# A spectral block with a gated MLP: an addition moved behind its copy, the weights' sums moved ahead of a multiplication, the banks read at the head of a step, and one transform stage a step later

## The chip, the cores and the metric

The kernel runs on one core of one Trainium2 chip. The metric is the device time of one execution in microseconds (us). Before the change it is 1405.28 us, the median of 3 runs (1405.17 to 1407.20).

## The reference

```python
xn = _layernorm(x, axis=-1)
return x + _A_ref(xn, A_w_r, A_w_i) + _B_ref(xn, B_w_gate, B_w_up, B_w_down)

# _A_ref: a global filter in the frequency domain
X = rfft2(x) * (w_r + 1j * w_i);  y = irfft2(X, s=(S, D))
# _B_ref: a gated MLP
h = sigmoid(x @ w_gate) * (x @ w_up);  return h @ w_down
```

x has S = 2048 rows and D = 576 columns, the MLP is F = 4608 wide, and all of it is in fp32. The kernel splits every fp32 operand of a multiplication into a high and a low part (in the type fp32r) for TensorE, and adds three partial products.

## The kernel before

The program has two large parts. The first computes h = sigmoid(xn Wg) * (xn Wu); the second computes h Wd and, beside it, the whole spectral branch.

**The units.** Both products with xn use Strassen's scheme with seven products in place of eight. A unit (f, p) handles one block of 128 columns of Wg and of Wu and one of the two halves p of the rows; f runs over 36 blocks. `unit` (line 388) is written in the order in which the engines get their work. A product (`prod`, line 355) is seven matmuls of 128x512. TensorE (PE) runs P5 into the bank pE, P6 into pB, P2 into pA, P7 into pB, P1 of the next unit into its own pA (`ahead`, line 384), P4 into pB and P3 into pE, which has two banks. ScalarE (ACT) reads between the products: the copy pB <- pA (line 396), the copy h[:,0] (line 400), the gate's sigmoid g[:,0] (line 403), the copy h[:,1] (line 406) and the second sigmoid (line 413). VectorE (DVE) adds pE to h[:,1] (line 410), later pE to h[:,0] (line 416), and multiplies h by g (line 417). P3 accumulates into the bank pE that the addition of line 410 reads, so P3 waits for that addition.

Seven times in a unit, between these steps, `beside` is called. It gives one step each to three generators of side work: `make_w`, which splits the next block's weights (ScalarE's copies on line 213, the low parts on lines 217 and 219) and forms the sums that Strassen's scheme needs (lines 229, 231, 232); `early`, for the last unit only, which fetches and splits the first operands of the second part; and the sides, which are `export` (line 420) and `make_t` (line 447). `export` forms the sums of h in place (lines 434 to 443) and stores them to a buffer in DRAM; `make_t` does the same for w_down (low parts on line 462). A unit with p = 0 uses weights that were split during the units before; in a unit with p = 1 the next block's weights are still being split. An instruction that waits holds back all that stands behind it on its engine.

**The product stage.** The second part is a list of 252 steps (line 1214 on): 7 products j, 2 halves p, and 18 blocks k of the sum. A step has twelve matmuls of 128x288 into the four banks m0 to m3 (`down`, line 1197). Ahead of them stand, in this order, a fetch of the operand of ten steps later, its split into a high part on ScalarE (`cut_hi`, line 795, four steps ahead of use) and a low part on DVE (`cut_lo`, line 799, three steps ahead), and `emptied`, which reads the banks of a finished product (`evac`, lines 1141 and 1145). When k comes to its end, the next product wants the same four banks.

**The spectral branch** runs beside these steps, as generators that get one step each in `aside`, behind the matmuls. `phase1b` (line 917) handles one block of 128 rows: it normalizes (xb, line 285), transposes on PE (pf, lines 940 and 941), copies out (fh, fl), multiplies (pd, line 962), copies out on ScalarE in four parts (ah) and subtracts on DVE (al), multiplies again (pa, line 975), copies out (x1, ScalarE) and stores x1 to DRAM. Sixteen blocks begin at the steps 2 + int(3.7 i), so three or four steps apart, and up to five are under way at a time. pf, pd and pa share two pairs of PSUM banks (tag pp); ah, al and x1 have one buffer each. The later phases use the same pairs.

From the third unit on the order on PE, DVE and ScalarE is the order of the program text; only the first two units are ordered by the framework. Line numbers below are those of the kernel before where nothing else is said.

Of the kernel before, what the change touches and what calls it, by code (L numbers as in the profile page):

```python
# [9 lines left out]
F32 = mybir.dt.float32  # L10
F32R = mybir.dt.float32r
I32 = mybir.dt.int32
AF = mybir.ActivationFunctionType
OP = mybir.AluOpType
PSUM = bass.MemoryType.PSUM

P = 128
# [107 lines left out]
def spectral_glu_kernel(ctx: ExitStack, tc: tile.TileContext, x, w_r, w_i, w_gate, w_up, w_down, out):  # L125
# [59 lines left out]
    def get_x(p, k):  # L185
        return X[p, HOME.get(k, k)]
# [20 lines left out]
    def weight(f, k):  # L207
        i, n = WPLACE[k]
        return WS[f, i][:, n]
# [142 lines left out]
    STEPS = ((0, 0), (3, 0), (0, 3), (1, 1), (4, 1), (1, 4), (2, 2))  # L352
    H = {}

    def prod(b, w, xx, start, stop, skip=False):
        for j, (sx, sw) in enumerate(STEPS):
            nc.tensor.matmul(b, w[:, sw, :], xx[:, sx, :], start=start and j == 0, stop=stop and j == len(STEPS) - 1,  # L357
                             skip_group_check=skip)

# [16 lines left out]

    B = {}

    def made(u, b, k, start, stop=True):
        f, p = u  # L380
        ka, kb = FACTORS[k]
        prod(B[u, b], weight(f, kb), get_x(p, ka), start, stop, not start)

    def ahead(u):
        B[u, "A"] = bank("bA", f"pA{u[0]}_{u[1]}", 2)
# [2 lines left out]
    def unit(u, beside, after):  # L388

        f, p = u  # L390
        h = new_h(f, p)
        g = run.tile([P, 2, CW], F32, tag="g", name=f"g{f}_{p}")
        B[u, "B"] = bank("bB", f"pB{f}_{p}")
        B[u, "E"] = bank("bE", f"pE{f}_{p}", 2)
        bA, bB, bE = (B[u, k] for k in "ABE")
        nc.scalar.activation(bB, bA, AF.Copy)
        made(u, "E", "P5", True)
        beside()
        made(u, "B", "P6", False)
        nc.scalar.activation(h[:, 0], bB, AF.Copy)  # L400
        beside()
        made(u, "A", "P2", False)
        nc.scalar.activation(g[:, 0], bA, AF.Sigmoid)
        beside()
        made(u, "B", "P7", False)
        nc.scalar.activation(h[:, 1], bB, AF.Copy)  # L406
        beside()
        if after:
            ahead(after)
        nc.vector.tensor_tensor(h[:, 1], h[:, 1], bE, op=OP.add)  # L410
        beside()
        made(u, "B", "P4", False)
        nc.scalar.activation(g[:, 1], bB, AF.Sigmoid)  # L413
        beside()
        made(u, "E", "P3", False)
        nc.vector.tensor_tensor(h[:, 0], h[:, 0], bE, op=OP.add)  # L416
        nc.vector.tensor_tensor(h, h, g, op=OP.mult)  # L417
        beside()

    def export(k, p):  # L420

        a, b = H[2 * k, p], H[2 * k + 1, p]
        A11, A21, A12, A22 = a[:, 0], a[:, 1], b[:, 0], b[:, 1]

        def put(what, src):
            nc.sync.dma_start(ssp[ORDER.index(what)][p][k], src)

        put("P1", A11)
        put("P2", A12)
        put("P4", A22)  # L430
        s = run.tile([P, 2, CW], F32, tag="s", name=f"s{k}_{p}")
        S1, S2 = (s[:, i] for i in range(2))
        yield
        nc.vector.tensor_tensor(S1, A21, A22, op=OP.add)
        put("P5", S1)
        yield
        nc.vector.tensor_tensor(S2, S1, A11, op=OP.subtract)
        put("P6", S2)
        yield
        nc.vector.tensor_tensor(A21, A11, A21, op=OP.subtract)  # L440
        put("P7", A21)
        yield
        nc.vector.tensor_tensor(A12, A12, S2, op=OP.subtract)
        put("P3", A12)
        yield

    def make_t(k):
# [353 lines left out]
    def early():  # L801
        for n in range(20):
            if n < 2:
                for i in range(3):
                    fetch(3 * n + i)
            else:
                fetch_t(0, n - 2)
            if 12 <= n <= 12 + CA:
                cut_hi(n - 12)
            if 13 <= n < 13 + CA:  # L810
                cut_lo(n - 13)
            yield
        for n in range(FS, FA):
            fetch(n)
# [5 lines left out]
    for i, u in enumerate(UNITS):  # L820
# [29 lines left out]

        unit(u, beside, after)
        if f % 2 == 1:
            sides.append(export(f // 2, p))
        if u == (3, 0):
            load_raw(4)
            load_raw(5)
# [60 lines left out]
    def phase1b(t):  # L917
# [50 lines left out]
        yield  # L968
        for o, sl, src in quarters:
            lo(al[o, sl, :], src, ah[o, sl, :])  # L970
        yield
        pa = pair(f"pa{t}")
        for sl in range(2):
# [232 lines left out]

    done, out_of = [], []

    def emptied():
        out_of[:] = [g for g in out_of if next(g, out_of) is not out_of]  # L1210
        out_of.extend(g for g in done if next(g, done) is not done)
        done.clear()

    for n, (j, p, k) in enumerate(seq):
        fetch(n + FA)
        for load in loads.pop(n, []):
            load()
        if n:
            cut_hi(n + CA)
            cut_lo(n + CA - 1)  # L1220
        emptied()
        if k in (0, NPR - 2):
            for m in range(2):
                down(n, m)
                down(n + 1, m)
        elif k in (1, NPR - 1):
            for m in range(2, TPC):
                down(n - 1, m)
                down(n, m)
        else:  # L1230
            for m in range(TPC):
                down(n, m)
        active.extend(b() for b in begin.pop(n, []))
        aside()
    while active or done or out_of:
        emptied()
        aside()
    assert not begin and not loads, (begin, loads)
    written.close()
# [22 lines left out]
```

## Time and profile before

| what | us |
|---|---|
| median of 3 runs | 1405.28 (1405.17 to 1407.20) |
| the profiled execution: its own time | 1405.81 |
| the profiled execution: span of the profile | 1403.9 |
| PE busy (share of the span) | 1379.7 (98%) |
| DVE busy | 967.0 (69%) |
| ScalarE (ACT) busy | 714.8 (51%) |

The span runs from the first to the last instruction that the profiler recorded; the execution's own time is 1.9 us longer. All traced times are places or durations in this one execution. A row of instructions gives the place where it starts, how long it takes, the engine, the line, the operation, the tiles that are written and read, the shape, and a count where several alike stand behind one another; in brackets stands the idle time of the engine just ahead of it and what ended it. A row of the waits gives the total, the number of waits and the longest. A row of windows gives the stretch, its length, the busy time of PE, PEld (the weight load), DVE, ScalarE, GpSimd and SyncE with the instructions in brackets, the granted clock of PE, the busy share of the transfer engines and GB/s.

### The profile page before, as it was taken

The numbers are of one execution on the slowest core, as the hardware profiler recorded it, in microseconds if no ns is written. First come the engines' busy times: TensorE is split into PE (matmuls) and PEld (weight loads), VectorE is DVE, ScalarE is ACT, GpSimd is POOL, SyncE is SP. The second block draws the span as 40 slices with busy tenths as digits, with TensorE's granted clock in tenths as the row PEclk, the third lists the DMA queues.
The fourth block names the chain that finished last, engine by engine and source line by source line (L and its number), as shares of the span: only waits on it lengthen the run. The fifth ranks groups of instructions, "written<-read, shape, count | busy, mean of one in ns | idle before, by whom it ended". The sixth has DMA issues, their size and how long they took to land.

```text
span 1403.9 us, 22607 instructions
## 1 busy us (share of the span) xinstructions
PE 1379.7 (98%) x7827; PEld 1220.9 (87%) x7827; DVE 967.0 (69%) x1807; ACT 714.8 (51%) x1469; POOL 12.7 (1%) x29
## 2 busy tenths in 40 slices
PE   9999999999999999999999999999999999999999
PEld 7778888788887888888788878999999999999998
DVE  8795677666866677666867665666757777756664
ACT  5564444444444444444444433655657767745553
POOL 2000000000000000000000000000000000000000
PEclk9999999999999999999999999999999999999999
DMA  7022565456554565545564439996899999988751
GB/s 242 23 99 92 181 215 206 159 172 211 188 206 147 188 206 206 178 168 204 187 208 157 169 143 335 329 331 216 257 293 276 308 282 306 306 284 278 246 189 62
DMA packets 221538, 296.77 MB, mean 211 GB/s; under 512 B 18544, under 2 KB 124400, under 8 KB 221168
## 3 DMA queue, kind: packets, MB, share of 16 engines
q1 hardware_dynamic: 221280, 295.26, 63.5%
q8 instruction: 62, 1.02, 0.3%
q14 instruction: 52, 0.43, 0.1%
q10 hardware_dynamic: 144, 0.07, 0.0%
HBM read 177.82 MB, written 117.44 MB: 210 GB/s over the span
## 4 chain that ended last, share of the span: by engine, by line
PE 86%; DVE 9%; issue 2%; DMA 2%; ACT 2%; DVEq 0%; ACTq 0%; SPq 0%
PE m L1203 26%; PE pB L357 21%; PE pE L357 15%; PE pA L357 14%; PE pd L962 2%; PE pe L1091 2%; PE py L1054 1%; PE pa L975 1%; PE pb L1006 1%; PE pc L1028 1%; DMA acc<-in_A_x 1%; DVE xs L323 1%; DVE raw L229 1%; DVE w L217 1%; PE pz L1069 0%
## 5 line engine op out<-in xcount | busy, mean ns | idle before, releaser
L1203 PE MATMUL m<-tt,sp 128*128 128x288 f32 x3024 | 415.9, 294 | 4.5 <-DVE u L1141 2.8
L1203 PEld LDWEIGHTS m<-tt,sp 128*128 128x128 f32 x3024 | 403.2, 188 | 5.8 <-DVE u L1141 3.5
L799 DVE TENSOR_TENSOR sp<-sf,sp 128x512 fp32r<-128x512 f32 x252 | 169.2, 688 | 24.4 <-ACT sp L795 22.1
L795 ACT ACTIVATE sp<-sf 128x512 fp32r<-128x512 f32 x252 | 155.2, 629 | 48.9 <-PE m L1203 25.7
L213 ACT ACTIVATE w<-raw 128x384 fp32r<-128x384 f32 x238 | 113.2, 515 | 99.8 <-DVE raw L229 98.8
L357 PE MATMUL pA<-X1A,w 128*128 128x512 f32 x518 | 129.2, 389 | 0.0
L357 PE MATMUL pE<-X1S,w 128*128 128x512 f32 x490 | 123.4, 392 | 4.2 <-DVE h L410 4.1
L416 DVE TENSOR_TENSOR h<-h,pE 128x512 f32<-128x512 f32 x68 | 46.8, 688 | 108.9 <-PE pE L357 108.8
L357 PE MATMUL pE<-X0S,w 128*128 128x512 f32 x483 | 121.1, 390 | 0.1
L357 PE MATMUL pB<-X1S,w 128*128 128x512 f32 x476 | 120.7, 393 | 0.1
L357 PE MATMUL pA<-X0A,w 128*128 128x512 f32 x483 | 120.8, 389 | 0.0
L357 PE MATMUL pB<-X0S,w 128*128 128x512 f32 x476 | 119.2, 390 | 1.0 <-ACT h L400 1.0
L357 PEld LDWEIGHTS pA<-X1A,w 128*128 128x128 f32 x518 | 97.2, 188 | 20.1
L357 PEld LDWEIGHTS pE<-X1S,w 128*128 128x128 f32 x490 | 91.1, 188 | 26.7 <-DVE h L410 8.0
L357 PEld LDWEIGHTS pB<-X1S,w 128*128 128x128 f32 x476 | 88.1, 188 | 23.3 <-ACT h L400 4.5
L357 PEld LDWEIGHTS pE<-X0S,w 128*128 128x128 f32 x483 | 90.4, 188 | 19.6 <-DVE w L217 0.5
L357 PEld LDWEIGHTS pA<-X0A,w 128*128 128x128 f32 x483 | 90.6, 188 | 18.9
L413 ACT ACTIVATE g<-pB 128x512 f32<-128x512 f32 x68 | 40.7, 598 | 130.0 <-PE pB L357 130.0
L357 PEld LDWEIGHTS pB<-X0S,w 128*128 128x128 f32 x476 | 89.2, 188 | 19.9 <-ACT h L400 1.4
L400 ACT ACTIVATE h<-pB 128x512 f32<-128x512 f32 x68 | 40.1, 589 | 120.9 <-PE pB L357 116.2
L410 DVE TENSOR_TENSOR h<-h,pE 128x512 f32<-128x512 f32 x68 | 46.6, 685 | 74.5 <-ACT h L406 74.5
L417 DVE TENSOR_TENSOR h<-h,g 128x1024 f32<-128x1024 f32 x68 | 83.3, 1225 | 7.4 <-DVE h L416 0.5
(206 smaller groups left out, 1907.3 us busy)
## 6 DMA issues: line engine op xcount, KB each, us to landing
sf<-ss SPq DMA_DIRECT2D x252, 256.0 KB
ss<-h SPq DMA_DIRECT2D x180, 256.0 KB
ts<-tP SPq DMA_DIRECT2D x126, 288.0 KB
tt<-ts SPq DMA_DIRECT2D x126, 288.0 KB
ss<-s SPq DMA_DIRECT2D x72, 256.0 KB
wd<-in_B_w_down SPq DMA_DIRECT2D x36, 288.0 KB
raw<-in_B_w_gate SPq DMA_DIRECT2D x72, 128.0 KB
raw<-in_B_w_up SPq DMA_DIRECT2D x72, 128.0 KB
```

Of the source, the lines that this page charges most:

```text
L213: nc.scalar.activation(o[:, i, :3, :], src[:, i], AF.Copy)
L357: nc.tensor.matmul(b, w[:, sw, :], xx[:, sx, :], start=start and j == 0, stop=stop and j == len(STEPS) - 1, skip_group_check=skip)
L400: nc.scalar.activation(h[:, 0], bB, AF.Copy)
L410: nc.vector.tensor_tensor(h[:, 1], h[:, 1], bE, op=OP.add)
L413: nc.scalar.activation(g[:, 1], bB, AF.Sigmoid)
L416: nc.vector.tensor_tensor(h[:, 0], h[:, 0], bE, op=OP.add)
L417: nc.vector.tensor_tensor(h, h, g, op=OP.mult)
L795: nc.scalar.activation(s[:, 0], SF[n], AF.Copy)
L799: nc.vector.tensor_tensor(SP_[n][:, 1], SF[n], f32(SP_[n][:, 0]), op=OP.subtract)
L962: nc.tensor.matmul(pd[:, e, :NQ], l, r, start=n == 0, stop=n == len(steps) - 1)
L1091: nc.tensor.matmul(pe[:, e, :NQ], l, r, start=n == 0, stop=n == len(steps) - 1)
L1203: nc.tensor.matmul(o, s[:, a, m * P:(m + 1) * P], t[:, b, :], start=k == 0 and i == 0, stop=k == NPR - 1 and i == 2)
```

## The change

In `unit` the addition to h[:,1] moves from behind P1 of the next unit to directly behind ScalarE's copy h[:,1], ahead of that place's `beside`. The seventh `beside` moves from behind the addition to h[:,0] and the multiplication to ahead of both, directly behind P3. In the last unit, which has no next one, P2 is split: four matmuls stand in its place, and the other three and the sigmoid g[:,0] stand behind P7, where other units have the next P1.

`export` of the last unit writes P3's operand into a tile of its own in place of h's buffer, and `early` splits one more low part. In the product stage the first step of a bank's reading (`read_out`) stands ahead of the step's `cut_hi` and `cut_lo`; the steps of readings that were begun earlier stay behind them. `phase1b` has one more step between al and pa. The line numbers of the changed kernel are up to 9 higher.

```diff
@@ -352,8 +352,9 @@
     STEPS = ((0, 0), (3, 0), (0, 3), (1, 1), (4, 1), (1, 4), (2, 2))
     H = {}
 
-    def prod(b, w, xx, start, stop, skip=False):
-        for j, (sx, sw) in enumerate(STEPS):
+    def prod(b, w, xx, start, stop, skip=False, which=range(len(STEPS))):
+        for j in which:
+            sx, sw = STEPS[j]
             nc.tensor.matmul(b, w[:, sw, :], xx[:, sx, :], start=start and j == 0, stop=stop and j == len(STEPS) - 1,
                              skip_group_check=skip)
 
@@ -376,10 +377,10 @@
 
     B = {}
 
-    def made(u, b, k, start, stop=True):
+    def made(u, b, k, start, stop=True, which=range(len(STEPS))):
         f, p = u
         ka, kb = FACTORS[k]
-        prod(B[u, b], weight(f, kb), get_x(p, ka), start, stop, not start)
+        prod(B[u, b], weight(f, kb), get_x(p, ka), start, stop, not start, which)
 
     def ahead(u):
         B[u, "A"] = bank("bA", f"pA{u[0]}_{u[1]}", 2)
@@ -399,25 +400,31 @@
         made(u, "B", "P6", False)
         nc.scalar.activation(h[:, 0], bB, AF.Copy)
         beside()
-        made(u, "A", "P2", False)
-        nc.scalar.activation(g[:, 0], bA, AF.Sigmoid)
+        if after:
+            made(u, "A", "P2", False)
+            nc.scalar.activation(g[:, 0], bA, AF.Sigmoid)
+        else:
+            made(u, "A", "P2", False, which=range(4))
         beside()
         made(u, "B", "P7", False)
         nc.scalar.activation(h[:, 1], bB, AF.Copy)
+        nc.vector.tensor_tensor(h[:, 1], h[:, 1], bE, op=OP.add)
         beside()
         if after:
             ahead(after)
-        nc.vector.tensor_tensor(h[:, 1], h[:, 1], bE, op=OP.add)
+        else:
+            made(u, "A", "P2", False, which=range(4, len(STEPS)))
+            nc.scalar.activation(g[:, 0], bA, AF.Sigmoid)
         beside()
         made(u, "B", "P4", False)
         nc.scalar.activation(g[:, 1], bB, AF.Sigmoid)
         beside()
         made(u, "E", "P3", False)
+        beside()
         nc.vector.tensor_tensor(h[:, 0], h[:, 0], bE, op=OP.add)
         nc.vector.tensor_tensor(h, h, g, op=OP.mult)
-        beside()
-
-    def export(k, p):
+
+    def export(k, p, apart=False):
 
         a, b = H[2 * k, p], H[2 * k + 1, p]
         A11, A21, A12, A22 = a[:, 0], a[:, 1], b[:, 0], b[:, 1]
@@ -440,8 +447,9 @@
         nc.vector.tensor_tensor(A21, A11, A21, op=OP.subtract)
         put("P7", A21)
         yield
-        nc.vector.tensor_tensor(A12, A12, S2, op=OP.subtract)
-        put("P3", A12)
+        o = run.tile([P, 2, CW], F32, tag="g", name=f"o{k}_{p}")[:, 0] if apart else A12
+        nc.vector.tensor_tensor(o, A12, S2, op=OP.subtract)
+        put("P3", o)
         yield
 
     def make_t(k):
@@ -807,7 +815,7 @@
                 fetch_t(0, n - 2)
             if 12 <= n <= 12 + CA:
                 cut_hi(n - 12)
-            if 13 <= n < 13 + CA:
+            if 13 <= n <= 13 + CA:
                 cut_lo(n - 13)
             yield
         for n in range(FS, FA):
@@ -850,7 +858,7 @@
 
         unit(u, beside, after)
         if f % 2 == 1:
-            sides.append(export(f // 2, p))
+            sides.append(export(f // 2, p, not after))
         if u == (3, 0):
             load_raw(4)
             load_raw(5)
@@ -968,6 +976,7 @@
         yield
         for o, sl, src in quarters:
             lo(al[o, sl, :], src, ah[o, sl, :])
+        yield
         yield
         pa = pair(f"pa{t}")
         for sl in range(2):
@@ -1206,19 +1215,24 @@
 
     done, out_of = [], []
 
-    def emptied():
-        out_of[:] = [g for g in out_of if next(g, out_of) is not out_of]
-        out_of.extend(g for g in done if next(g, done) is not done)
+    def read_out():
+        fresh = [g for g in done if next(g, done) is not done]
         done.clear()
+        return fresh
+
+    def emptied(fresh):
+        out_of[:] = [g for g in out_of if next(g, out_of) is not out_of] + fresh
 
     for n, (j, p, k) in enumerate(seq):
         fetch(n + FA)
         for load in loads.pop(n, []):
             load()
+        fresh = read_out()
         if n:
             cut_hi(n + CA)
+        if n > 1:
             cut_lo(n + CA - 1)
-        emptied()
+        emptied(fresh)
         if k in (0, NPR - 2):
             for m in range(2):
                 down(n, m)
@@ -1233,7 +1247,7 @@
         active.extend(b() for b in begin.pop(n, []))
         aside()
     while active or done or out_of:
-        emptied()
+        emptied(read_out())
         aside()
     assert not begin and not loads, (begin, loads)
     written.close()
```

What DVE has behind a unit with p = 0 and in the unit with p = 1 that follows it: h_0_2010 is the first unit's h, raw are the weights of the next block, and the sums of lines 229, 231 and 232 are those for which ScalarE's copies wait. Before:

```order
L217 TENSOR_TENSOR w_6_2042<-raw_1915,w_6_2042 128x3x256
L219 TENSOR_TENSOR w_6_2042<-raw_1915,w_6_2042 32x3x128
L416 TENSOR_TENSOR h_0_2010<-h_0_2010,pE_0_2013 128x512
L417 TENSOR_TENSOR h_0_2010<-h_0_2010,g_0_2011 128x1024
L229 TENSOR_TENSOR raw_1915<-raw_1915 128x2x384
L231 TENSOR_TENSOR raw_1915<-raw_1915 128x384
L232 TENSOR_TENSOR raw_1915<-raw_1915 128x384
L462 TENSOR_TENSOR tP_2113<-wd_2044,tP_2113 128x288
```

and now:

```order
L217 TENSOR_TENSOR w_6_2042<-raw_1915,w_6_2042 128x3x256
L219 TENSOR_TENSOR w_6_2042<-raw_1915,w_6_2042 32x3x128
L229 TENSOR_TENSOR raw_1915<-raw_1915 128x2x384
L424 TENSOR_TENSOR h_0_2010<-h_0_2010,pE_0_2013 128x512
L425 TENSOR_TENSOR h_0_2010<-h_0_2010,g_0_2011 128x1024
L231 TENSOR_TENSOR raw_1915<-raw_1915 128x384
L232 TENSOR_TENSOR raw_1915<-raw_1915 128x384
L470 TENSOR_TENSOR tP_2113<-wd_2044,tP_2113 128x288
```

The first sum of the weights has moved ahead of the addition to h[:,0] (line 416, now 424) and of the multiplication (417, now 425). Further on in the same unit with p = 1, whose h is h_1_2096, the rows up to its addition to h[:,0]; w_6 is a low part of the weights, s_0 and h_0 belong to an export, tP to `make_t`. Before:

```order
L437 TENSOR_TENSOR s_0_2118<-s_0_2118,h_0_1822 128x512
L217 TENSOR_TENSOR w_6_2127<-raw_1915,w_6_2127 128x2x256
L219 TENSOR_TENSOR w_6_2127<-raw_1915,w_6_2127 32x2x128
L462 TENSOR_TENSOR tP_2144<-wd_2046,tP_2144 128x288
L440 TENSOR_TENSOR h_0_1822<-h_0_1822 128x512
L410 TENSOR_TENSOR h_1_2096<-h_1_2096,pE_1_2099 128x512
L443 TENSOR_TENSOR h_0_2010<-h_0_2010,s_0_2118 128x512
L416 TENSOR_TENSOR h_1_2096<-h_1_2096,pE_1_2099 128x512
```

and now:

```order
L444 TENSOR_TENSOR s_0_2118<-s_0_2118,h_0_1822 128x512
L411 TENSOR_TENSOR h_1_2096<-h_1_2096,pE_1_2099 128x512
L217 TENSOR_TENSOR w_6_2127<-raw_1915,w_6_2127 128x2x256
L219 TENSOR_TENSOR w_6_2127<-raw_1915,w_6_2127 32x2x128
L470 TENSOR_TENSOR tP_2144<-wd_2046,tP_2144 128x288
L447 TENSOR_TENSOR h_0_1822<-h_0_1822 128x512
L451 TENSOR_TENSOR h_0_2010<-h_0_2010,s_0_2118 128x512
L470 TENSOR_TENSOR tP_2181<-wd_2046,tP_2181 128x288
L424 TENSOR_TENSOR h_1_2096<-h_1_2096,pE_1_2099 128x512
```

The addition to h[:,1] (line 410, now 411) has moved ahead of two rows of the low part, one row of `make_t` and one of the export (line 440, now 447). In the product stage, PE at the first place where blocks of the spectral branch are three steps apart: pd1 is the second product's bank pair of block 1, pa0 that of the third product of block 0, pf2 the transposes of block 2, and m0_11 is a bank of the product stage. Before, pa0 stands in the step before and so ahead of these rows:

```order
L962 MATMUL pd1_8182<-cf_7780,fh1_8114 128x290
L962 MATMUL pd1_8182<-cf_7780,fr1_8116 128x290
L1203 MATMUL m0_10_8207<-tt0_0_7578,sp18_8054 128x288 x3
L1203 MATMUL m0_10_8207<-tt0_1_7580,sp19_8093 128x288 x3
L1203 MATMUL m0_11_8214<-tt0_0_7578,sp18_8054 128x288 x3
L1203 MATMUL m0_11_8214<-tt0_1_7580,sp19_8093 128x288 x3
L940 MATMUL pf2_8230<-idr_58,eo2_8120 128x128 x2
L941 MATMUL pf2_8230<-idr_58,rp2_8149 99x128
L940 MATMUL pf2_8230<-idr_58,eo2_8120 128x128 x2
```

and now:

```order
L1212 MATMUL m0_11_8208<-tt0_0_7578,sp18_8055 128x288 x3
L1212 MATMUL m0_11_8208<-tt0_1_7580,sp19_8094 128x288 x3
L984 MATMUL pa0_8215<-ah0_8109,am0_8048 128x290
L984 MATMUL pa0_8215<-al0_8110,am0_8048 128x290
L984 MATMUL pa0_8215<-ah0_8109,am0_8048 128x290 x2
L984 MATMUL pa0_8215<-al0_8110,am0_8048 128x290
L984 MATMUL pa0_8215<-ah0_8109,am0_8048 128x290
L948 MATMUL pf2_8228<-idr_58,eo2_8121 128x128 x2
L949 MATMUL pf2_8228<-idr_58,rp2_8150 99x128
L948 MATMUL pf2_8228<-idr_58,eo2_8121 128x128 x2
L949 MATMUL pf2_8228<-idr_58,rp2_8150 99x128
L1212 MATMUL m0_12_8240<-tt0_0_7578,sp18_8055 128x288 x3
```

pa0 has moved from ahead of pd1 to directly ahead of pf2. ScalarE at the same place; x10 is the copy out of pa0, ah1 the four copies out of pd1, fh2 the copy out of pf2, sp a cut of the product stage and u03 a bank's reading. Before:

```order
L1145 ACTIVATE u03_8205<-m0_03_7795 128x288
L905 ACTIVATE x10_8221<-pa0_8175 128x2x290
L905 ACTIVATE ah1_8224<-pd1_8182 64x290 x4
L795 ACTIVATE sp23_8239<-sf23_8029 128x512
L905 ACTIVATE fh2_8260<-pf2_8230 128x512
```

and now:

```order
L1154 ACTIVATE u03_8196<-m0_03_7796 128x288
L803 ACTIVATE sp22_8198<-sf22_8003 128x512
L913 ACTIVATE ah1_8222<-pd1_8176 64x290 x4
L803 ACTIVATE sp23_8237<-sf23_8030 128x512
L913 ACTIVATE x10_8254<-pa0_8215 128x2x290
L913 ACTIVATE fh2_8261<-pf2_8228 128x512
```

The copy out of pa0 has moved from ahead of the four copies out of pd1 to behind them and behind one cut.

## The prediction

> **What bounds the kernel now.** I read the page's head and its first part, then the list of PE's waits, then the lines that are waited for (409 to 411, 400, 1141), then timelines around single waits.
>
> ```profile
> span 1403.9 us, 22607 instructions
> PE 1379.7 (98%) x7827; PEld 1220.9 (87%) x7827; DVE 967.0 (69%) x1807; ACT 714.8 (51%) x1469; POOL 12.7 (1%) x29
> ```
>
> TensorE is busy for 98% of the span and every other engine has slack, so an edit is worth only what it takes from PE's gaps, 24.2 us in all. The list of PE's waits says whose they are (total us, times, longest):
>
> ```profile
> PE pE L357 <- DVE h L410: 4.1, 6, 1.2
> ...
> PE m L1203 <- DVE u L1141: 2.8, 3, 1.4
> ...
> PE m L1203 <- DVE sp L799: 1.1, 1, 1.1
> ...
> PE m L1203 <- DVE acc L1141: 0.6, 1, 0.6
> ```
>
> The change goes for these four and for two waits on the bank pB. A record of idle time is shorter than the loss, since matmuls are pipelined; so I price each wait from start to start.
>
> **The change part by part.**
>
> *h's addition behind its copy.* P3 writes into the bank that this addition (L410) reads. One of the waits, on PE:
>
> ```profile
> 450.94 1.75 PE L357 MATMUL pA<-X0A,w 128*128 128x512 f32 x7
> 452.53 1.75 PE L357 MATMUL pB<-X1A,w 128*128 128x512 f32 x7
> 455.44 1.90 PE L357 MATMUL pE<-X1S,w 128*128 128x512 f32 x7 [1.16 <-DVE h L410]
> 457.18 1.77 PE L357 MATMUL pE<-X0S,w 128*128 128x512 f32 x7
> ```
> ```profile
>   PEld pE L357: 8.4, 10
> ```
>
> An undisturbed product takes 1.59 (450.94 to 452.53). Here P3 starts 2.91 after P4, and the next product 1.74 after P3: 1.32 + 0.15 = 1.47 lost, 0.31 more than the idle shown. The second row (who waited for L410) counts ten waits of weight loads, so ten losses, four of them too short to show on PE: 4.1 + 10 x 0.31 = 7.2. In the new place one low part of the weights, an export step and a step of make_t run behind the addition and not ahead of it, and the addition is ready more than two products before P3. What it holds back on DVE (the low part w2, 1.1 us) is wanted by P6 of the next unit, over 4 us later. I count 7.2 gone; if the cover failed in the fullest units, 1 to 2 would stay.
>
> *Sums of the weights ahead of the last multiplication.* In a half-1 unit ScalarE's copies of the weights wait for L229, and the copy h (L400) stands behind them:
>
> ```profile
> 560.97 0.94 ACT L213 ACTIVATE w<-raw 128x384 fp32r<-128x384 f32 x2 [3.29 <-DVE raw L229]
> 561.02 1.75 PE L357 MATMUL pA<-X1A,w 128*128 128x512 f32 x7
> ...
> 562.78 1.89 PE L357 MATMUL pB<-X1S,w 128*128 128x512 f32 x7
> ...
> 564.51 1.76 PE L357 MATMUL pA<-X0A,w 128*128 128x512 f32 x7
> ```
> ```profile
>   PEld pB L357: 5.9, 12
> ```
>
> P7 starts 1.76 after P2, and the next product 1.73 later: 0.17 + 0.14 = 0.31. The second row (who waited for L400) has twelve; ten look like this, one per half-1 unit that is late: 10 x 0.31 = 3.1. With L229 ahead of the multiplication ScalarE, idle 3.29 here, copies some 2 us sooner: 3.1 gone. The multiplication comes up to 1.4 later where DVE is behind, and is awaited (by the gate's sigmoid) two products further on: no cost.
>
> *Last unit and last export.* The rows of the last P4, of the last export's in-place subtraction (L443) and of what waits for it, and the transfers' share (last column but one of the windows view):
>
> ```profile
> 856.38 1.75 PE L357 MATMUL pB<-X1S,w 128*128 128x512 f32 x7
> 858.82 1.88 PE L357 MATMUL pB<-X1A,w 128*128 128x512 f32 x7 [0.69 <-ACT h L406]
> ```
> ```profile
> 868.65 0.69 DVE L443 TENSOR_TENSOR h<-h,s 128x512 f32<-128x512 f32 x1 [2.26 <-DMA ss<-h]
> ...
> 870.00 12.64 PE L1203 MATMUL m<-tt,sp 128*128 128x288 f32 x94 [1.14 <-DVE sp L799]
> ```
> ```profile
> 866.00:868.00 2.00, 2.00 (x17) 2.00 (x16) 0.40 (x1) 1.26 (x2) 0.00 (x0) 1.00 1.05 404
> 868.00:870.00 2.00, 0.87 (x7) 0.63 (x6) 1.35 (x3) 0.63 (x1) 0.00 (x0) 1.00 0.71 271
> 870.00:872.00 2.00, 2.00 (x15) 2.00 (x16) 2.00 (x4) 0.00 (x0) 0.00 (x0) 1.00 0.82 262
> ```
> ```profile
> 885.01 0.58 DVE L285 TENSOR_SCALAR xb<-acc,mv,rstd 128x576 f32<-128x576 f32 x1 [4.81 <-DMA acc<-in_A_x]
> ```
>
> P4 starts 2.44 after P7, not 1.59; three matmuls of P2 (0.68) now fill most of the 0.85: 0.7. The subtraction into a buffer of its own waits for no store, and cut_lo(4) comes before it: about 1.4 at 870.00. But the transfer engines are full before and after (1.05), and a DVE step at 885.01 waits for one of them, with pd of the first block behind it. Only the dip at 868 to 872 (0.29 x 2 + 0.18 x 2 = 0.9) can be made up there. So between 0.9 and 2.1; I take 1.3, nearer to the transfers.
>
> *Banks read first.* Beside the rows on L1141 above, one of the four:
>
> ```profile
> 1098.89 0.69 DVE L799 TENSOR_TENSOR sp<-sf,sp 128x512 fp32r<-128x512 f32 x1
> 1099.49 0.82 DVE L1141 TENSOR_TENSOR acc<-acc,u 128x288 f32<-128x288 f32 x2
> 1100.23 0.81 DVE L1141 TENSOR_TENSOR u<-u,m 128x288 f32<-128x288 f32 x2
> ```
> ```profile
> 1098.82 1.22 PE L1203 MATMUL m<-tt,sp 128*128 128x288 f32 x8
> 1100.73 3.56 PE L1203 MATMUL m<-tt,sp 128*128 128x288 f32 x25 [0.69 <-DVE u L1141]
> ```
>
> The reads of the banks stand behind 1.3 us of work that nobody awaits and now stand ahead of it; all four waits should go. Eight matmuls at 0.13 (914.41 to 914.54 below) end at 1099.86, so 0.87 is lost where 0.69 shows, and about 0.1 more at the restart: 2.8 + 0.6 + 4 x 0.28 = 4.5. One of the four loses the cover of pa_15, which moves behind it: 4.3.
>
> *s1 transform a step later.* What goes first, with what follows it on PE and ScalarE:
>
> ```profile
> 910.03 3.38 PE L1203 MATMUL m<-tt,sp 128*128 128x288 f32 x24
> 913.65 0.37 PE L975 MATMUL pa<-ah,am 128*128 128x290 f32 x1 [0.24 <-PE m L1203]
> ...
> 914.41 0.30 PE L975 MATMUL pa<-ah,am 128*128 128x290 f32 x1
> 914.54 0.69 PE L1203 MATMUL m<-tt,sp 128*128 128x288 f32 x4
> ```
> ```profile
> 909.86 0.63 ACT L795 ACTIVATE sp<-sf 128x512 fp32r<-128x512 f32 x1
> ...
> 914.79 0.66 ACT L905 ACTIVATE x<-pa 128x580 f32<-128x580 f32 x1 [2.08 <-issue]
> ...
> 918.28 1.68 ACT L905 ACTIVATE ah<-pd 64x290 fp32r<-64x290 f32 x4 [2.31 <-issue]
> 919.99 0.60 ACT L905 ACTIVATE fh<-pf 128x512 fp32r<-128x512 f32 x1
> ```
>
> 24 matmuls at 0.13 take 3.12, and pa comes after 3.62: 0.5, in four blocks 2.0, and a step later this is gone: -2.0. But the move makes a new wait. Blocks start 3 or 4 steps apart. Where it is 3 (blocks 0, 3, 10, 6 and 13), pa_t now stands in the step in which ScalarE copies the next block's ah, and directly ahead of the pf of the block after that. ah has one buffer, so these four copies wait for pa_t's last matmul. Of the two pairs of banks one holds the pd whose low half DVE reads only a step later, so pf must take pa_t's, and waits for its copy x1; ScalarE has that copy behind the four of ah and one cut. After pa_t's last matmul starts: 0.30 until its end, 0.09 to ScalarE's start (914.71 to 914.79), 1.68 for ah, 0.03, 0.63 for the cut, 0.03, 0.66 for x1, 0.05 to PE = 3.47, where 0.13 is usual: 3.34, and 0.04 at the restart: 3.38. Five times: +16.9. All that DVE, ScalarE and SP do in the stall is ahead of need afterwards, so it isn't paid twice.
>
> *The clock.* A stall of 3.3 us may also slow PE after it. The trace has one such place (windows with PE's busy time second and the granted clock, PEclk, last but two), and the seven matmuls that run in it:
>
> ```profile
> 59.00:63.20 4.20, 2.59 (x12) 1.25 (x12) 2.01 (x7) 2.57 (x7) 0.00 (x0) 0.97 0.17 62
> 63.20:66.60 3.40, 3.40 (x11) 2.65 (x11) 2.84 (x7) 1.55 (x4) 0.00 (x0) 0.53 0.00 0
> ```
> ```profile
> 63.27 3.27 PE L357 MATMUL pE<-X1A,w 128*128 128x512 f32 x7
> ```
>
> After 4.2 us with PE 2.59 busy the granted clock was 0.53 for 3.4 us, and seven matmuls took 1.52 longer than the 1.75 at 450.94. The idle 1.16 at 455.44 was followed by 1.77 for seven: no drop. A stall with nothing at all for 3.3 us is nearer to the first; depending on where it falls it may stay unnoticed. Bounds: none of five (0) and all five (5 x 1.52 = 7.6); I take three, +4.6.
>
> [...]
>
> **The sum.** -7.2 - 3.1 - 1.3 - 4.3 - 2.0 = -17.9; +16.9 + 4.6 = +21.5; together +3.6. The profiled execution took 1405.81 (span 1403.9, 1.9 around it), 0.5 above the median of 1405.28: 1409.4 on its scale, 1408.9 on the median's.
>
> **The rivals.**
>
> *The clock holds.* The five stalls are there and cost only themselves: 1405.28 - 17.9 + 16.9 = 1404.3, not slower. For it: each stall is short by itself, and PE is 98% busy around it. Against it: the drop at 63.2 came after less darkness. The point that decides is whether PEclk falls below 1.00 between 890 and 1035. [...] Chance 0.22.
>
> *The clock drops after all five.* 1404.3 + 7.6 = 1411.9. Chance 0.13, with room for an addition to h that still comes late.
>
> *The copies aren't held.* If ScalarE had x1 ahead of the four copies, each stall would be 0.30 + 0.09 + 0.66 + 0.05 - 0.13 = 1.0, and 1405.28 - 17.9 + 5 = 1392.4: faster by 0.9%. Against it: the order of ScalarE in the changed program, with ah, cut, x1 in that row, and ah's single buffer. The same figure, within some us, stands for any mistake of mine by which pf does not wait. Chance 0.08.
>
> *The waits only move.* The addition is early, but DVE then holds what is awaited next, as L229's copies or the banks; half of 17.9 comes back, 1404.3 + 9 = 1413, before any drop of the clock. DVE is busy 69% by the first row quoted, so this is unlikely: 0.05.
>
> **How the numbers follow.** The forecast, five stalls and the clock dropping after some of them, has 0.52, from 1406 to 1411. The range, 1403.6 to 1412.4, takes in the first rival and most of the second and leaves out the third and the fourth. A measurement here tells 0.2%, 2.8 us, from no change: 1402.5 to 1408.1. Slower by more: two thirds of the forecast, the second and the fourth rival, 0.53. Within: the rest of the forecast and the first rival, 0.38. Faster: the third, and an edge of the first, 0.09.
>
> **What would show it.** Right: in the list of PE's waits no row from h's addition, from u or acc, or from sp at 870; PE's waits for x from ScalarE at pf, five of about 3.2 us, at four or five places between 890 and 1035; between them PEclk at half for stretches of 3.4 us. The unit stage shorter by some 10 us, the stage of s1 longer by 15 to 23. Wrong: no row of pf waiting for x, or rows of under 1 us (third rival); PEclk at 1.00 throughout (first); pE still waiting for h, or new waits on pB or m of over 2 us (fourth).

## The result and the profile after

The changed kernel takes 1414.89 us (median of 7 runs, 1411.58 to 1416.74), the kernel before 1405.66 in the same comparison: a ratio of 1.0059, 95% interval 1.0047 to 1.0072. One of the seven executions of the kernel before took 2776.82 and is left out of the ratio. The change is slower, as forecast, but by 8.3 us by that ratio (9.2 by the two medians) where 3.6 was said, and the median lies 2.5 above the range.

The profiled execution is the fastest of the seven (1411.58). Its head and first part:

```profile
span 1409.7 us, 22612 instructions
PE 1377.3 (98%) x7827; PEld 1225.9 (87%) x7827; DVE 966.3 (69%) x1807; ACT 720.6 (51%) x1469; POOL 12.8 (1%) x29
```

PE's busy share reads as before, 98%, and so tells nothing. The list of its waits does (total us, times, longest):

```profile
PE pf L948 <- ACT x L913: 15.7, 5, 3.1
PE pc L1037 <- DVE zl L916: 2.1, 2, 1.3
...
PE py L1063 <- issue: 1.1, 2, 0.5
...
PE m L1212 <- DVE acc L1150: 0.5, 1, 0.5
```

Of the four rows shown of before three are gone (pE for h, m for u, m for sp), and m for acc shrank from 0.6 to 0.5. Three rows are new. The first is the forecast stall, five times, 3.1 at most. The two below it were not forecast: PE waits in the later stages for zl and at py, both behind VectorE (for py the profile names no releaser; at 1276.88 it starts 0.10 after VectorE's last reading of pe, whose pair of banks it takes). The timeline at the first stall shows the mechanism as the prediction has it:

```profile
888.06 0.29 PE L984 MATMUL pa<-ah,am 128*128 128x290 f32 x1
...
888.45 1.67 ACT L913 ACTIVATE ah<-pd 64x290 fp32r<-64x290 f32 x4 [3.37 <-issue]
890.14 0.63 ACT L803 ACTIVATE sp<-sf 128x512 fp32r<-128x512 f32 x1
...
890.79 0.66 ACT L913 ACTIVATE x<-pa 128x580 f32<-128x580 f32 x1
...
891.50 0.69 PE L948 MATMUL pf<-idr,eo 128*128 128x128 f32 x2 [3.14 <-ACT x L913]
```

From the start of pa's last matmul (888.06) to pf (891.50) are 3.44, forecast 3.47. ScalarE stood idle for 3.37 ahead of ah, then did four copies, a cut and only then the copy that PE waits for.

The granted clock around this stall and around the second, by windows of 3.41 (PE's busy time second, the clock last but two):

```profile
887.67:891.08 3.41, 0.69 (x6) 0.45 (x4) 0.91 (x3) 2.55 (x6) 0.00 (x0) 1.00 0.95 340
891.08:894.50 3.42, 3.00 (x14) 3.00 (x15) 3.21 (x7) 1.24 (x3) 0.00 (x0) 0.50 0.79 245
894.50:897.91 3.41, 3.41 (x28) 3.41 (x28) 2.42 (x5) 2.08 (x5) 0.00 (x0) 1.00 0.90 259
918.39:921.80 3.41, 1.92 (x15) 1.68 (x13) 0.00 (x0) 1.37 (x4) 0.00 (x0) 1.00 1.02 347
921.80:925.21 3.41, 1.76 (x15) 1.76 (x16) 2.94 (x7) 2.49 (x6) 0.00 (x0) 1.00 0.93 316
```

Behind the first stall the clock was at half for 3.41; behind the other four, equally long, it stayed at 1.00. There is one more difference near the start: the drop that the kernel before has at 62.95 for one window lasts two in this execution.

```profile
62.95:66.37 3.42, 3.25 (x9) 2.50 (x9) 3.07 (x7) 1.80 (x4) 0.00 (x0) 0.50 0.00 0
```
```profile
61.65:65.06 3.41, 3.05 (x9) 2.00 (x10) 2.40 (x7) 2.60 (x7) 0.00 (x0) 0.50 0.00 0
65.06:68.47 3.41, 3.41 (x15) 2.86 (x14) 2.54 (x5) 0.58 (x2) 0.00 (x0) 0.50 0.00 0
```

The first row is of the kernel before, the other two are of the changed kernel. Experiment 1's kernel, whose first part is the changed kernel's, has one window there in its trace, and experiment 2's, whose first part is that of before, has two; so this is no effect of the change.

The seven executions have mean clocks of 0.992 to 0.996 with their times in nearly the same order (1416.74 at 0.992, 1411.58 and 1412.27 at 0.996), and the kernel before has mostly 0.998 or 0.999.

Two questions stood behind that: whether the 4.7 us too few in the sum are the clock or something else, and what decides that the clock falls.

### The profile page after: what moved, and what is told of

Its sections match the earlier page's. It is cut to its first block, busy times and chain, and to the rows that moved or that the text cites. A ratio compares the mean times of both kernels' runs of the same rounds, so it can differ in the third digit from the quotient of the medians.

```text
span 1409.7 us, 22612 instructions
## 1 busy us (share of the span) xinstructions
PE 1377.3 (98%) x7827; PEld 1225.9 (87%) x7827; DVE 966.3 (69%) x1807; ACT 720.6 (51%) x1469; POOL 12.8 (1%) x29
## 4 chain that ended last, share of the span: by engine, by line
PE 87%; DVE 4%; DMA 3%; issue 3%; ACT 2%; SPq 1%; ACTq 0%; DVEq 0%
PE m L1212 24%; PE pB L358 22%; PE pE L358 15%; PE pA L358 15%; PE pe L1100 2%; PE pd L970 2%; DMA tt<-ts 1%; PE py L1063 1%; PE pc L1037 1%; PE pb L1015 1%; DMA ss<-s 1%; PE warmpr L602 1%; PE pa L984 1%; DMA acc<-in_A_x 1%; PE pA L572 1%
## 5 line engine op out<-in xcount | busy, mean ns | idle before, releaser
L411 DVE TENSOR_TENSOR h<-h,pE 128x512 f32<-128x512 f32 x68 | 46.8, 688 | 147.5 <-ACT h L410 141.9
L217 DVE TENSOR_TENSOR w<-raw,w 128x512 fp32r<-128x512 f32 (+2 forms) x108 | 82.3, 762 | 6.3 <-ACT w L213 5.4
```

The costliest lines, as they stand in the source:

```text
L217: nc.vector.tensor_tensor(o[:, :, 3:, :], src[:, :, :KT, :], f32(o[:, :, :KT, :]), op=OP.subtract)
```

## The experiments

To compare the experiments with each other, I multiply each ratio by 1405.66; the intervals of the ratios are plus or minus 0.0013 to 0.0016, or about 2 us. Theory A is the prediction's: the added step makes five stalls, each may be followed by a drop of the clock. Theory B is that drops and spread have other causes in the change.

**1. The change without the added step.**

```diff
         for o, sl, src in quarters:
             lo(al[o, sl, :], src, ah[o, sl, :])
         yield
-        yield
         pa = pair(f"pa{t}")
```

> The changed kernel without the added step between al and pa; all else as changed. Theory A (the extra step makes five stalls of 3.30 us, and the clock falls to half behind one to five of them, another number in each execution): the profiled 1411.58 of the changed kernel, minus 16.5 for the stalls, minus 1.2 for its one drop of the clock at 892, plus 1.9 for the four waits of pa that come back: 1395.8, with all executions within 2 us of each other. Theory B (the drops of the clock and the spread of 5 us have nothing to do with the stalls): 1397 to 1400, and the spread stays.

Measured: 1393.64 (1392.98 to 1394.10), ratio 0.9908 (0.9895 to 0.9922), on the common scale 1392.7. The wait of pf is gone, and the spread of 5 us with it. Theory A holds, with the time 2 to 3 below the 1395.8 expected: that figure was worked out from the profiled execution and took away only its drop at the first stall, not its second window near the start. The rest of the change is worth 0.9%, and the added step costs 1.0059 x 1405.66 - 1392.7 = 1414.0 - 1392.7 = 21.3.

**2. The kernel before with the added step alone** (the same line, added to the kernel before).

> The kernel before with the added step alone. Theory A: 1405.66 + 16.5 - 1.9 + three or four drops of 1.3 = 1424.2 to 1425.5, single executions from 1421.6 (one drop) to 1426.8 (five), granted clock 0.992 to 0.997. Theory B: 1420.3 with the spread of before, clock 0.999.

Measured: 1431.32 (1430.21 to 1432.49), ratio 1.0176 (1.0163 to 1.0190), clock 0.989 or 0.990. The five waits of pf are 15.7 again, so the same stalls, but the time is 6 above what I expected. The windows at the fourth stall say why:

```profile
1007.07:1010.48 3.41, 1.19 (x9) 0.95 (x8) 1.33 (x3) 2.08 (x5) 0.00 (x0) 1.00 0.75 214
1010.48:1013.90 3.42, 2.50 (x12) 2.51 (x13) 3.22 (x8) 1.98 (x5) 0.00 (x0) 0.50 0.80 276
1013.90:1017.31 3.41, 3.41 (x16) 3.41 (x16) 2.52 (x6) 1.18 (x4) 0.00 (x0) 0.50 0.06 8
1017.31:1020.72 3.41, 3.41 (x28) 3.41 (x27) 0.28 (x1) 0.81 (x2) 0.00 (x0) 1.00 0.97 317
```

This drop lasts two windows. In this execution the clock fell behind all five stalls, three times for 3.41 and twice for 6.8: seven windows. Of 0.0176 x 1405.66 = 24.7 the stalls are 16.5 and the four waits of pa that go -1.6, which leaves 9.8. Of this, 1.3 are longer waits at the banks (in this trace m waits 1.6 for sp and 1.4 for acc, where before it was 1.1 and 0.6). So the clock took about 8.5, or 1.2 per window.

**3. Two buffers for ah and al.**

```diff
-        ah, al = wide(pool, "ah", t, 1, F32R), wide(pool, "al", t, 1, F32R)
+        ah, al = wide(pool, "ah", t, 2, F32R), wide(pool, "al", t, 1, F32R)
```

(al keeps its one buffer; the text on record names both.)

> The changed kernel with two buffers for ah (and al) in place of one, so that the four copies out of pd need not wait for pa; the order of all engines stays. Theory A (it is ah's one buffer that holds ScalarE): five stalls of 0.30 + 0.09 + 0.66 + 0.05 - 0.13 = 1.0 in place of 3.3, no drop of the clock: 1411.58 - 5 x 2.3 - 1.2 = 1398.9, spread under 2 us. Rival (the order of ScalarE alone, with the cut ahead of the copy x1, makes the stall): stalls of 3.3 stay, 1411 to 1417.

Measured: 1397.43 (1396.64 to 1398.57), ratio 0.9936 (0.9924 to 0.9949), clock 0.997 or 0.998. The order of every engine is the changed kernel's, and its waits of PE have this row:

```profile
PE pf L948 <- ACT x L913: 3.9, 5, 0.8
```

From 3.1 to 0.8 at most: what held ScalarE was ah's single buffer, the order alone costs 0.95 from start to start. With the stall the drops of the clock went too: its trace has the clock at 1.00 from 70 to 1396.

**4. The new readings behind the cuts** (the first experiment's kernel, with this):

```diff
-        fresh = read_out()
         if n:
             cut_hi(n + CA)
         if n > 1:
             cut_lo(n + CA - 1)
-        emptied(fresh)
+        emptied(read_out())
```

> The kernel of the first experiment (no added step) with the banks read behind the two cuts again, as before the change. Theory A (the two waits of pc for zl, 2.5 us, are what DVE owes when the banks are read first): the waits for u and acc come back, +3.0, those for zl go, -2.5: 0.5 slower than the first experiment, 1396.3. Rival (zl is late for another reason): 3.0 slower, 1398.8, with the waits for zl still there.

Both expectations missed: 1391.18 (1390.08 to 1391.88), ratio 0.9893 (0.9877 to 0.9908), 1390.6 on the common scale: 2.1 faster than the first experiment by the centres, which the intervals alone don't separate; the two traces do. The waits for u did not come back, because this edit leaves one part of the change in: a new reading still stands ahead of the later steps of older ones. And the waits for zl shrank, and the row of py is gone. Its VectorE in the stage where the last large one was, first the kernel of experiment 1, then of experiment 4:

```profile
1119.11 0.81 DVE L1149 TENSOR_TENSOR u<-u,m 128x288 f32<-128x288 f32 x2
1119.84 0.68 DVE L807 TENSOR_TENSOR sp<-sf,sp 128x512 fp32r<-128x512 f32 x1
1120.44 1.55 DVE L1149 TENSOR_TENSOR acc<-acc,u 128x288 f32<-128x288 f32 x4
1121.91 0.75 DVE L1026 TENSOR_TENSOR z<-z,t 128x578 f32<-128x578 f32 x1
1122.59 0.68 DVE L807 TENSOR_TENSOR sp<-sf,sp 128x512 fp32r<-128x512 f32 x1
1123.19 1.55 DVE L1149 TENSOR_TENSOR acc<-acc,u 128x288 f32<-128x288 f32 x4
1124.66 0.68 DVE L807 TENSOR_TENSOR sp<-sf,sp 128x512 fp32r<-128x512 f32 x1
1125.27 0.75 DVE L916 TENSOR_TENSOR zl<-z,zh 128x578 fp32r<-128x578 f32 x1
```
```profile
1117.38 0.68 DVE L807 TENSOR_TENSOR sp<-sf,sp 128x512 fp32r<-128x512 f32 x1
1117.99 0.81 DVE L1149 TENSOR_TENSOR u<-u,m 128x288 f32<-128x288 f32 x2
1118.72 1.55 DVE L1149 TENSOR_TENSOR acc<-acc,u 128x288 f32<-128x288 f32 x4
1120.19 0.75 DVE L1026 TENSOR_TENSOR z<-z,t 128x578 f32<-128x578 f32 x1
1120.86 0.68 DVE L807 TENSOR_TENSOR sp<-sf,sp 128x512 fp32r<-128x512 f32 x1
1121.46 1.55 DVE L1149 TENSOR_TENSOR acc<-acc,u 128x288 f32<-128x288 f32 x4
1122.94 0.68 DVE L807 TENSOR_TENSOR sp<-sf,sp 128x512 fp32r<-128x512 f32 x1
1123.54 0.75 DVE L916 TENSOR_TENSOR zl<-z,zh 128x578 fp32r<-128x578 f32 x1
```

VectorE has no gap in either. From the reading u to zl are 6.16 in the first (three cuts between) and 5.55 in the second (two): one cut of 0.61, moved behind the reading, makes zl later by just that, and PE waits for zl. The row of PE's waits in the second, which was 2.1 in the first as in the changed kernel:

```profile
PE pc L1036 <- DVE zl L916: 0.9, 2, 0.7
```

**5. The whole bank order of before, without the added step.**

```diff
-        fresh = read_out()
         if n:
             cut_hi(n + CA)
         if n > 1:
             cut_lo(n + CA - 1)
-        emptied(fresh)
+        out_of[:] = [g for g in out_of if next(g, out_of) is not out_of]
+        out_of.extend(read_out())
...
```

> No added step in s1, and the whole of the bank order of before: the two cuts, then the later steps of readings begun earlier, then the first step of a new reading. Left of the change are the units, the last export and the early cut. Theory A2 (what frees the banks early is that a new reading stands ahead of the later steps of older ones; that it stands ahead of the cuts gives nothing): the four waits for u and acc come back, +4.1 to 4.5, the waits of pc for zl go, -1.3: 1391.2 + 3.0 = 1394.2. That is also 1406.39 - 7.0 - 2.9 - 0.7 - 1.4 = 1394.4 from before. Rival (the place of the readings doesn't matter to the time): 1391.

Measured: 1393.18 (1393.13 to 1394.57), ratio 0.9909 (0.9894 to 0.9924), 1392.9 on the common scale. PE's waits have these rows again, and none for zl:

```profile
PE m L1211 <- DVE u L1149: 2.8, 3, 1.4
...
PE m L1211 <- DVE acc L1149: 0.6, 1, 0.6
```

So the change's bank order moved PE's waits from u to zl and py and gained nothing (0.9908 with it, 0.9909 without). Against experiment 4 it is 2.3, forecast 3.0.

**6. The later steps of the readings behind the spectral branch's work** (experiment 4's kernel):

```diff
-        emptied(read_out())
+        fresh = read_out()
...
         active.extend(b() for b in begin.pop(n, []))
         aside()
+        emptied(fresh)
```

> The kernel of the fourth experiment (cuts, then new readings), with the later steps of the readings moved behind the step's work of the spectral branch. Theory A2 (zl is late because four to eight additions into acc, which nobody awaits, stand ahead of it on VectorE): the waits of pc for zl, 1.26, go, the banks stay free of waits: 1389.9. Rival (these additions then hold back the next step's low cut, and the wait moves to sp): 1391 to 1393 with a wait of m for sp.

Measured: 1390.55 (1389.72 to 1391.57), ratio 0.9888 (0.9873 to 0.9903): 0.7 below experiment 4, within the interval. The waits for zl are the same 0.9 as there, but the edit doesn't test the additions: in its trace both groups of four still stand ahead of zl, only z now stands ahead of the first, and from u to zl it is 5.55 as in experiment 4. The traces show why 0.9 stay. From the first matmul of pb, ahead of the bank's reading, to the end of zl it is 11.46 here and in experiment 4, and 11.47 in experiment 5, where PE waits 1.43 for u in between and then not at all for zl. Without that wait PE comes to zl sooner, and zl is no sooner.

**7. The stalls shorter by the cut.** ScalarE's cut goes behind the first block's step of the branch:

```diff
-    def aside():
-        active[:] = [g for g in active if next(g, active) is not active]
+    def aside(cut=lambda: None):
+        kept = []
+        for i, g in enumerate(active):
+            if next(g, active) is not active:
+                kept.append(g)
+            if i == 0:
+                cut()
+        if not active:
+            cut()
+        active[:] = kept
...
-        if n:
-            cut_hi(n + CA)
...
-        aside()
+        aside(lambda: cut_hi(n + CA) if n else None)
```

> The changed kernel with cut_hi issued behind the first block's step of the spectral branch in place of ahead of all, so that ScalarE has ah, x1, cut in the place of ah, cut, x1: the five stalls are shorter by the cut, 3.30 - 0.66 = 2.65. Theory A (the clock falls only behind a stall of nearly 3.4 us): no drop, granted clock 0.998, 1410.3 - 5 x 0.66 = 1407.0, spread under 2 us. Rival (any stall of some us can let it fall, by its place in time): clock 0.992 to 0.997 still, 1408 to 1414.

Measured: 1422.26 (1421.44 to 1422.45), ratio 1.0114 (1.0097 to 1.0130), clock 0.993 or 0.994. The time is no test, since the moved cut makes waits of its own in the last stage (py waits 3.8 for z3r and 2.1 for sp). The stalls are 2.65 as meant, and the clock is the answer. At the second stall and the third:

```profile
915.68:919.09 3.41, 1.55 (x12) 1.31 (x10) 0.08 (x1) 1.72 (x5) 0.00 (x0) 1.00 1.02 351
919.09:922.50 3.41, 2.79 (x23) 2.79 (x24) 3.23 (x8) 2.47 (x5) 0.00 (x0) 1.00 1.00 321
946.39:949.80 3.41, 0.93 (x7) 0.69 (x7) 0.84 (x2) 2.49 (x6) 0.00 (x0) 1.00 0.81 207
949.80:953.22 3.42, 3.42 (x17) 3.42 (x17) 3.22 (x8) 2.11 (x6) 0.00 (x0) 0.50 0.30 101
```

It fell behind two of the five stalls of 2.65, at 949.81 and 1021.49 (the mean clock of 0.994 over a span of 1419.6 stands for about five windows at half, so it fell elsewhere too). So theory A, no drop behind stalls of 2.65, is wrong, and the other three, equally long, had none: the place in time decided, as the rival has it.

**8. The stalls longer**, by x1 copied three times over.

```diff
-        hi(x1, pa[:, :, :NQ])
+        for _ in range(3):
+            hi(x1, pa[:, :, :NQ])
```

> The changed kernel with the copy x1 made three times in a row (the same values), so that the five stalls are longer by two copies of 0.63 to 0.66: about 4.6. Theory A (a longer stall always holds a whole dark window): the clock falls behind all five in every execution, each for 3.4 to 6.8 us: 1410.3 + 5 x 1.3 + 5 x (1.5 to 3.0) = 1424.3 to 1431.8, spread under 3 us, clock 0.988 to 0.991. Rival (a drop depends on the place in time, not on the length): clock 0.992 to 0.997, 1418.3 to 1424.

Measured: 1426.14 (1425.84 to 1428.32), ratio 1.0144 (1.0129 to 1.0159), clock 0.986 to 0.988. The five stalls are 3.96, not 4.6 (pf waits for al by then), and four shorter ones of 0.47 stand between them. The clock fell behind all five, each time for two windows:

```profile
1032.39:1035.80 3.41, 1.23 (x10) 0.99 (x8) 0.40 (x1) 2.04 (x5) 0.00 (x0) 1.00 0.89 277
1035.80:1039.22 3.42, 1.80 (x9) 1.83 (x10) 2.12 (x5) 2.65 (x5) 0.00 (x0) 0.50 0.20 75
1039.22:1042.63 3.41, 3.41 (x16) 3.41 (x15) 1.52 (x3) 1.55 (x4) 0.00 (x0) 0.50 0.52 143
1042.63:1046.04 3.41, 3.41 (x28) 3.41 (x27) 0.47 (x1) 0.63 (x1) 0.00 (x0) 1.00 0.84 268
```

**9. The added step only where it makes no stall** (experiment 6's kernel).

```diff
+        if late:
+            yield
         pa = pair(f"pa{t}")
...
+            more = dict(late=int((i + 1) * rate) - int(i * rate) > 3) if phase is phase1b else {}
...
```

> The kernel of the sixth experiment with the added step in s1 only for those blocks whose next one begins four steps later. Theory A (the stall is made only where the next block begins three steps later, and the four waits of pa for al are at blocks with four): no wait of pf for x1, no wait of pa for al, 1.9 less than the sixth: 1388.7. Rival (any added step makes pf wait for x1): at least four stalls of 1 to 3.3, 1393 or more.

Measured: 1389.29 (1388.23 to 1389.86), ratio 0.9878 (0.9862 to 0.9893). Between 865 and 1035 only one wait of PE is left (m for acc, 0.6): no wait of pa, none of pf. So the added step costs no stall at blocks with four steps to the next, and the five stalls come from those with three. The gain of 1.4 over experiment 6 lies within the intervals; that the waits of pa are gone is in the trace. This is the fastest version by its median, 1.2% below the kernel before and 1.8% below the changed one.

**10. A stall of 1.6.** The third experiment's two buffers, with x1 copied twice over.

```diff
-        hi(x1, pa[:, :, :NQ])
+        for _ in range(2):
+            hi(x1, pa[:, :, :NQ])
```

> The changed kernel with two buffers for ah and the copy x1 made twice: five stalls of 0.95 + 0.65 = 1.6. Theory C (the clock is judged in windows of 3.41 us that lie on a fixed grid, and falls where PE is idle for 0.6 of one; 0.55 was not enough): 1.6 is 0.47 of a window, so no drop in any execution: 1397.43 + 5 x 0.65 = 1400.7, spread under 2 us, clock 0.998. Rival (the chance of a drop only grows with the length of the stall): a drop here and there, clock 0.996 or 0.997 in some executions, each 1.5 to 3 more.

Measured: 1402.02 (1401.15 to 1402.26), ratio 0.9967 (0.9955 to 0.9980), clock 0.997 or 0.998; the five waits of pf are 1.6 from start to start, and with that clock, the same as in experiment 3, nothing shows of a drop behind them. So Theory C, which the expectation states, is not refuted; a wait of at most 1.5 idle, the longest here, leaves PE some 1.9 of a window of 3.41 by my estimate, and behind the stalls the clock had fallen only after 1.38 or less, so this run doesn't come near that.

**11. The units alone** (on the kernel before).

```diff
         nc.scalar.activation(h[:, 1], bB, AF.Copy)
+        nc.vector.tensor_tensor(h[:, 1], h[:, 1], bE, op=OP.add)
         beside()
         if after:
             ahead(after)
-        nc.vector.tensor_tensor(h[:, 1], h[:, 1], bE, op=OP.add)
...
         made(u, "E", "P3", False)
+        beside()
         nc.vector.tensor_tensor(h[:, 0], h[:, 0], bE, op=OP.add)
         nc.vector.tensor_tensor(h, h, g, op=OP.mult)
-        beside()
```

> The kernel before with the two moves in the units alone (the addition to h[:,1] behind its copy; the seventh step of the side work ahead of the addition to h[:,0] and the multiplication). Theory A (the terms of the units are as the trace of the changed kernel shows them, 6.95 and 2.86): 1405.77 - 9.8 = 1396.0, no wait of pE for h, none of pB for the copy on line 400 in later units. Rival (half of it comes back where VectorE is late): 1400 to 1401.

Measured: 1395.84 (1393.93 to 1396.67), ratio 0.9923 (0.9911 to 0.9936), 1394.8 on the common scale. There is no wait of pE for h.

## Where the prediction was right and where it failed

Each term of the sum, with the runs that measure it (a difference of two runs is uncertain by some 2 to 3 us, a row from waits by far less):

| term | forecast | measured | from |
|---|---|---|---|
| units: h's addition, weights' sums | -7.2 - 3.1 | -10.9 | experiment 11 |
| last unit and last export | -1.3 | -1.9 | 5 less 11 |
| banks read first | -4.3 | -0.2 | 1 less 5 |
| the wait at the banks that the added step uncovers | in the -4.3 | +0.7 | 0.66 in the trace of the changed kernel, none in 1 |
| s1's waits of pa | -2.0 | -1.6 | four waits of 0.40 in the trace of 1 |
| five stalls | +16.9 | +16.5 | 5 x 3.30 from start to start |
| the clock | +4.6 | +5.7 | what is left of 21.3 |
| sum | +3.6 | +8.3 | |

**Right.** The units and the stalls. The stall was read from two orders (pa directly ahead of pf on PE; ah, cut, x1 on ScalarE) and priced within 3%, and experiment 3 shows its cause. The new place of h's addition and of the weights' sums delayed nothing that PE waits for.

**Failed: the bank term, by 4.8.** The step said that the reads stood "behind 1.3 us of work that nobody awaits and now stand ahead of it; all four waits should go". Three are down to 0.12 each (from start to start, in experiment 1's trace), and the one that loses the cover of pa is left at 0.66 in the changed kernel's. But the work is awaited: VectorE has no gap around the last reading, so what is put behind it makes zl late, and PE waits at pc 2.46 and at py 0.90 more (from start to start) in place of 4.1 at the banks. By these waits it is 3.7 for 4.1, which agrees with the difference of -0.2 between the runs. The prediction had this as its fourth rival, "the waits only move", and gave it 0.05 on the ground that VectorE is busy 69% of the whole span. That is the share of the span, and even the share of that stage hides it (107.70 of the 145 us from 1035 to 1180, 74%, before): where the last of the readings lies, the timelines in experiment 4 show no gap on VectorE for 6.9 us each. A smaller mistake lies in the same step: two things had moved, the reading past the cuts and the reading past older readings' later steps. Only the second frees the banks (experiment 4), and only the first makes zl later. This term's miss is as large as the whole miss of 4.7; that the others cancel to 0.1 is luck.

**Failed: the clock's bounds.** The term itself is 1.1 off, less than a difference of two runs can tell. Three drops of 1.52 were taken, with all five as the upper bound, 7.6. A drop was priced as one window, since the one example in the trace of before lasted 3.4; but in experiment 2 two of the five lasted two windows, where PE was busy for 2.30 and 2.50 in the first, and about 8.5 were lost behind the same five stalls. So the upper end of the range had to be some 0.9 higher for this alone. The single drop that it was priced from stands near the start, among other matmuls, where the clock fell after a window with 2.21 of PE's work, and behind the stalls only after 1.38 or less (last section). The length of a stall alone did not decide: with stalls of 2.65 the clock fell behind two of five in one execution (experiment 7), and behind five equal ones of 3.30 once in the changed kernel's profiled execution.

The profiled execution, 1411.58, holds one window at half speed behind the stalls and two near the start. The mean clock of the median one, 0.993 over a span of 1413.0, is a loss of 9.9 or nearly six windows at half; less one or two near the start it stands for some four or five behind the stalls, so most of the rest up to 1414.89 can be seen only in the executions' clocks. That each of the seven owes its time to its drops is therefore argued from the clock figures, not shown window by window.

## What to carry to other kernels

Before work is moved behind something on an engine that runs in the order of the program, ask whether that engine has a gap between this place and what is awaited next (here VectorE had none, and one cut of 0.61 made zl later by 0.61): a share of the whole span, or of a stage, doesn't say. A tile with one buffer ties its writer to its last reader (here PE's longest wait was 3.1 with one buffer for ah and 0.8 with two); when a step is made later, check which engine's queue then stands at that writer and whether anything awaited is behind it. And the stalls on PE had a second price here, the lower clock behind them: five of 3.30, together 16.5, became some 22 in the changed kernel and 25 in experiment 2, while five of 0.95 (experiment 3) had no drop behind them.

## What the runs showed of the hardware

In these traces the starts of the drops lie whole multiples of 3.413 us apart: in the changed kernel 243 from 61.65 to 891.08, in experiment 2, counted from the first stall's, 0, 9, 19, 31 and 41, counted likewise 0 and 21 in experiment 7 (949.81 and 1021.49) and 0, 10, 20, 33 and 43 in experiment 8. Laid on that grid, PE's busy time in a window of 3.41 goes with the clock of the next one: behind the stalls it fell to half after 0.33, 1.19 and 1.38 (experiment 2), 0.69 (the changed kernel), 0.93 (experiment 7) and 1.23 (experiment 8), and did not after 1.54, 1.76 and 1.92 (the changed kernel) and 1.55 (experiment 7). So at these stalls the border lies between 1.38 and 1.54, that is, 0.40 and 0.45 of a window. At half, a window with 3.00 (the changed kernel) brought it back, windows with 2.50 (experiment 2) and 1.80 (experiment 8) kept it there, so here that border lies between 0.73 and 0.88. The first stall of the changed kernel, 3.1 by its idle time, left PE 0.69 of one window, and the clock fell; the second, as long, lay astride two windows with 1.92 and 1.76, and it did not.

Near the start it doesn't fit. In the kernel before PE was busy for 2.21 of the 3.41 us ahead of its drop at 62.95, and in the changed kernel a window at half with 3.05 (61.65 to 65.06) was followed by a second one. The matmuls in the first of these stretches, and many in the second, were multiplications by the identity (pq and pr), that is, transposes; what lets the clock fall there was not shown.
